# Reordered start of a fused attention and expert kernel: GpSimd's first low half, the maxima of head 1, the gate copy and some routing operations

## Chip, core and metric

One core of a Trainium2 chip runs the whole kernel in one launch. The metric is the device time of one execution in microseconds (us); lower is better.

## What is computed

The reference has three stages: attention with a hashed mask, a mixture of 8 experts with one expert per token and a capacity, and a dense layer with a gated activation.

```python
B, H, S, D = 2, 8, 768, 64
mask = q_bucket[:, :, :, None] == k_bucket[:, :, None, :]   # 6 sign bits of q @ proj, k @ proj
scores = where(mask, q @ k.T / sqrt(D), -1e9)
attn = softmax(scores)
x = (attn @ v)                                              # 1536 tokens x 512
expert = argmax(x @ w_gate); gate = softmax(x @ w_gate)[expert]
y = gate * (relu(x @ w1[expert]) @ w2[expert])              # 512 -> 1024 -> 512, first `cap` tokens
h = y @ w_in                                                # 512 -> 2048
out = (h * clip(h + 3, 0, 6) / 6) @ w_out                   # 2048 -> 512
```

## The kernel before

The order of the work on every engine is written out by hand: instructions stand in each engine's queue in the order in which the program issues them, and each waits for its own operands. Factors are split into a high and a low part (fp16 or a rounded fp32), so a product is a sum of two or three matmuls.

**Attention.** There are 16 heads, each with 6 blocks of 128 keys, so 96 steps `k`. `mx(n)` (L448 to L461) takes two matmuls into one of three PSUM buffers `psm`, each followed on VectorE by a maximum (L457) over 384 keys; after the sixth block of a head, L460 reduces to `top`, and SyncE sends it by DMA into row 76 of `X` (L461), where the scores of that head read it. `scores(k)` (L463) takes four matmuls (L471, L472) into two buffers `pst` and two exponentials on ScalarE (L473) into `pf`. `high(k)` rounds `pf` to fp16 `phi` on ScalarE or VectorE; `low(k)` (L487) subtracts it from `pf` on GpSimd or VectorE to give `plo`. `pv` (L502 to L504) multiplies by the values, 18 matmuls for a block, two blocks in every odd step. A head's maxima run ahead of its scores by some steps: `Q["ac"]` gives how many are issued in each of the first steps (through `AHEAD`).

**The start (ramp).** Before the main loop stand head 0's maxima, the first two score blocks and `vscale(0)` (L601 to L643), a chain of small VectorE operations with two tiny TensorE products in it, which finds the power-of-two scales of the values and of the gate weights. Its last operation writes `isw` (L643). `vsplit(h)` (L715) splits the values of a head: ScalarE L721 and L723, then GpSimd L727 for heads 0 and 1 and VectorE L729 for later ones. `vgate(r)` (L557) brings the products of two heads' values with the gate weights: matmuls into `psg` (L565), a copy to `gv` (L571), two transposes (L575), and four small VectorE operations (L583, L584). `low_half` (L372) is VectorE's low part of a head's queries and keys. `heat` (L335) issues 512-column matmuls whose result nobody reads; `Q["hn"]` tells how many in each of the first steps. `stages(gen, ks)` runs the successive parts of a piece of work at the given times: a part with time `t` is issued by `due`, which is called with `k - 0.5` at the start of step `k` and with `k` at its end.

**The end of attention.** The last maxima are issued in step 87. `route(0)` (L208) and `weigh(0)` (L277), the routing of the first batch's tokens, are spread in 22 and 7 parts among the steps from 66 on: `pos` (L248), `ge` (L251), a count and `jo` (L253, L254), `pl` and `jt` (L257, L259), `rh` (L204), then the one-hot blocks `ohr` (L273).

**Behind attention.** The routing of the second batch, 8 experts (L1099, L1126) and the dense layer (L1348, L1375) follow; nothing of them is changed.

Of the kernel before, what the change touches and what calls it, by code (L numbers as in the profile page):

```python
# [23 lines left out]
NC = S // P  # L24
# [39 lines left out]
def moe_attention_kernel(ctx, tc, qk, v, vt, pj, wg, w1, w2, win, wout, out, cap):  # L64
    nc = tc.nc
    pe, act, dve, pool, sp = nc.tensor, nc.scalar, nc.vector, nc.gpsimd, nc.sync
# [3 lines left out]
    def opened(stack, name, bufs, side="left", **kw):  # L70
        return stack.enter_context(tc.tile_pool(name=name, bufs=bufs, side=side, reuse_waits="tile", **kw))
# [4 lines left out]
    def run(gen):  # L76
        for _ in gen:
            pass
# [4 lines left out]
    def persist(shape, dt, name):  # L83
        return const.tile(shape, dt, tag=name, name=name)
# [14 lines left out]
    isw = persist([P, 1], F32, "isw")  # L99
# [208 lines left out]
                )  # L308


    Q = {'tk': (84, 86), 'v': (-3.25, -4.75, -1.75, -2.25), 'vg': (-6.5, -6.75), 'vgd': 1, 'pr': (-13.0, -12.75, -12.0, -12.5), 'prd': 0.6, 'b0': 7.75, 'b': 1.75, 'bd': 0.5, 'vm0': (9.5, 10.5, 11.5, 12.5), 'vm': (-0.5, 4.75, 7.0, 12.25), 'vs': 13.25, 'pa': 1.5, 'ev': 0.5, 'lvt': -5.0, 'v4': (2.0, 4.25, 10.0, 16.25), 'vg0': (1.85, -4.4, 9.0), 'p2': 3.5, 'lr': (0.25, 1.25, 2.25), 'lv': 4.0, 'vsd': 0.75, 'ac': (1, 1, 3, 5, 6, 7, 8, 10), 'hd': (3, 5, 17), 'hn': (0, 0, 3, 2, 2, 1, 0, 0), 'ap': (0,), 'h0': (7,), 'hl': (6,), 'l0': (), 'll': (1, 3), 'ht': (6, 3, 7, 6, 3, 2)}


    HT = Q["ht"]

    with ExitStack() as actx:
        pa = opened(actx, "pa", 1)
        pr = opened(actx, "pr", 6)
# [4 lines left out]
        ps_v = opened(actx, "ps_v", 2, space=PSUM)  # L323
# [6 lines left out]
        def heat(pool_, tag, n, cols=512):  # L330

            if pool_ not in heat_t:
                heat_t[pool_] = pool_.tile([P, 512], F32, tag=tag, name=f"heat{tag}")
            for _ in range(n):
                pe.matmul(heat_t[pool_][:, :cols], idle_sb[:, 0:P], idle_sb[:, :cols], start=True, stop=True)  # L335
# [19 lines left out]
        def misc(name):  # L355
            return ps_x.tile([P, 512], F32, tag="x", name=name)
# [121 lines left out]
        def high(k, eng):  # L478
            phi_t[k] = pt.tile([P, S], F16, tag="phi", name=f"phi{k}", bufs=6)
            if eng is act:  # L480
                act.activation(phi_t[k], pf_t[k], AF.Copy)  # L481
            else:
                eng.tensor_copy(phi_t[k], pf_t[k])

        def low(k, eng):
            plo_t[k] = pt.tile([P, S], F16, tag="plo", name=f"plo{k}", bufs=5)
            eng.tensor_tensor(out=plo_t[k], in0=pf_t.pop(k), in1=phi_t[k], op=ALU.subtract)  # L487
            if k in Q["tk"]:
                c = plo_t[k][:, 0:1]
# [111 lines left out]
        def vscale(g, fresh=misc):  # L601

            am = am_t.pop(g)
            n = 1 + (g == 0)
            am1 = ph.tile([P, n], F32, tag="am1", name=f"am1{g}")
            dve.tensor_reduce(out=am1[:, 0:1], in_=am, axis=AX.X, op=ALU.max)
            if n > 1:
                dve.tensor_reduce(
                    out=am1[:, 1:2], in_=wg_sb.rearrange("p k h e -> p (k h e)"), axis=AX.X, op=ALU.max,
                    apply_absolute_value=True,  # L610
                )
            yield
            ps = misc(f"psn{g}")
            pe.transpose(ps[0:n, 0:P], am1, ident)
            yield
            am2 = ph.tile([n, 1], F32, tag=f"am2{n}", name=f"am2{g}")
            dve.tensor_reduce(out=am2, in_=ps[0:n, 0:P], axis=AX.X, op=ALU.max)
            if n > 1:
                a, am2 = am2, ph.tile([n, n], F32, tag="dg", name="dg")
                dve.tensor_tensor(out=am2, in0=a.to_broadcast([n, n]), in1=ident[0:n, 0:n], op=ALU.mult)  # L620
            yield
            ps = misc(f"pso{g}")
            pe.matmul(ps[:, 0:n], ones[0:n, :], am2, start=True, stop=True)
            yield

            a = ph.tile([P, n], F32, tag=f"am3{n}", name=f"am3{g}")
            dve.tensor_copy(a, ps[:, 0:n])
            a = a.bitcast(I32)
            x = ph.tile([P, 2 * n - 1], I32, tag=f"ex{n}", name=f"ex{g}")
            sc = sc_t[g] = ph.tile([P, 2 * n - 1], F32, tag=f"sc{n}", name=f"sc{g}", bufs=1 + (n == 1))  # L630
            dve.tensor_scalar(out=a, in0=a, scalar1=23, scalar2=None, op0=ALU.logical_shift_right)
            dve.tensor_scalar(out=a, in0=a, scalar1=15, scalar2=None, op0=ALU.max)
            for i, (j, k, c) in enumerate(((0, -1, 268), (1, -1, 268), (1, 1, 7))[: 2 * n - 1]):
                dve.tensor_scalar(
                    out=x[:, i : i + 1], in0=a[:, j : j + 1], scalar1=k, scalar2=c, op0=ALU.mult, op1=ALU.add
                )
            dve.tensor_scalar(out=sc.bitcast(I32), in0=x, scalar1=23, scalar2=None, op0=ALU.logical_shift_left)
            dve.tensor_copy(vsc[:, g : g + 1], sc[:, 0:1])
            sw_t[g] = ph.tile([P, 1], F32, tag="sw", name=f"sw{g}", bufs=2)
            dve.tensor_scalar(out=sw_t[g], in0=sc[:, 0:1], scalar1=SW, scalar2=None, op0=ALU.mult)  # L640
            if n > 1:
                dve.tensor_scalar(out=wg_sb, in0=wg_sb, scalar1=sc[:, 1:2], scalar2=None, op0=ALU.mult)
                dve.tensor_copy(isw, sc[:, 2:3])  # L643
# [131 lines left out]
        b0 = bits(0, [ps_v.tile([P, 512], F32, tag="v", name=f"psb0{n}") for n in range(2)])  # L775
# [9 lines left out]
        vs = vscale(0)  # L785
# [7 lines left out]
        next(vs)  # L793
        next(vs)
        run(vs)
        heat(ps_v, "v", 2)
        mx(NC)
        run(pre[1])
# [2 lines left out]
        first = vsplit(0), vgate(0)  # L801
# [4 lines left out]
        STEPS = NC * NH  # L806
        AC = (1,) + Q["ac"]
        AHEAD = [range(NC + AC[i], NC + AC[i + 1]) for i in range(8)]
        END = 2 * NC

        def on_dve(k):
            if k < END:
                return k in Q["h0"]
            return k - STEPS + END in Q["hl"] if k >= STEPS - END else k % 24 in Q["hd"]

        def on_pool(k):
            if k < END:
                return k not in Q["l0"]
            return k < STEPS - END or k - STEPS + END in Q["ll"]
# [4 lines left out]
        def at(k, f, *args):  # L824
            later.setdefault(k, []).append((f, args))

        def spread(k, gen, d=1):


            def part(k):  # L830
                if next(gen, gen) is not gen:
                    n = k + (d if k < STEPS - NC * 2 else min(d, 1) * 0.75)
                    at(n, part, n)

            at(k, part, k)

        def stages(gen, ks):
            for k in ks:
                at(k, next, gen, None)

        stages(first[0], (2, 2))
        stages(first[1], (2, 3, 3.5, 4, 4.5))
        at(5.0, run, pre[2])
        for i in range(3):
            at(Q["lr"][i], load_r, 5 + i)
        for g in range(1, G):
            b = 4 * NC * (g - 1)
            spread(b + Q["b"] + (g == 2) if g > 1 else Q["b0"], bits(g), Q["bd"])
            at(b - 6 if g > 1 else Q["lv"], load_v, g)
            for i in range(4):  # L850
                at(b + (Q["vm"] if g > 1 else Q["vm0"])[i], vmax, g, i)
            if g == 1:
                stages(vscale(g), (13, 14.5, 15.25, 16.75, 17.5))
            else:
                spread(b + Q["vs"], vscale(g))
        for h in range(8, NH):
# [8 lines left out]
        for h in range(NH):  # L865
            k = NC * h + NC - 1 + LAG
# [5 lines left out]
            elif h < NH - 1:  # L872
                at(k + Q["pa"], pair, h // 2)
                at(NC * h + (Q["lvt"] if h > 1 else -3.5), load_vt, h // 2 + 1)
        stages(route(0, lambda: misc("psr0")), [66 + 1.5 * i for i in range(8)] + [84.5 + 0.75 * i for i in range(14)])
        stages(weigh(0), (84, 86, 87.25, 88.5, 90.5, 91.5, 92.5))
        stages(any_unmatched(), (88.5, 91, 93.5))
        for i in range(4):
# [10 lines left out]
        for k in range(STEPS + LAG + 2):  # L889
            due(k - 0.5)  # L890
            if 1 < k <= STEPS and not on_dve(k - 1):
                high(k - 1, act)
            if 1 < k < STEPS:
                scores(k)
            if k < 8 and Q["hn"][k]:
                heat(ps_v, "v", Q["hn"][k])
            u = k - 2
            if 0 <= u < STEPS:
                if u not in phi_t:
                    high(u, dve)  # L900
                low(u, pool if on_pool(u) else dve)
            for n in AHEAD[k] if k < len(AHEAD) else (k + LEAD,):
                if n < STEPS:
                    mx(n)
            for u in (k - LAG - 1, k - LAG) if k % 2 else ():
                if 0 <= u < STEPS:
                    pv(u)
            due(k)
# [664 lines left out]
```

## Time and profile before

| what | value |
|---|---|
| runs of the kernel before | 659.13, 660.0, 663.14 us (median 660.0) |
| the profiled execution, its own time | 659.11 us |
| span of the profile | 657.4 us |
| mean granted TensorE clock in the span | 0.987 of full |
| attention steps in the span | from about 15 to 223 us |

The span is counted from the profile's first instruction; all times below are us from there. PE is TensorE, PEld its weight loads, DVE VectorE, ACT ScalarE, POOL GpSimd, SP the queue of SyncE. A row of the timeline gives start, duration, engine, line, operation, output and inputs, the number of instructions merged into the row, and in brackets the idle time of the engine before it with what ended it. The duration of merged rows covers all of them.

### The profile page before, as it was taken

What the parts mean: (1) busy time and instruction counts of PE and PEld (TensorE: products, weight loads), DVE (VectorE), ACT (ScalarE), POOL (GpSimd) and SP (SyncE); (2) the same over time, 40 slices, a digit from 0 to 9 for tenths busy, and PEclk for the clock granted to TensorE, in tenths of its full rate; (3) what the DMA queues carried; (4) which work ended last, traced back from release to release, by engine and by line L of the source; (5) the groups of instructions that cost most, each with busy time, mean ns of one, the idle gap of its engine ahead of it and who ended that gap; (6) DMA issues with size and microseconds to landing.
All of it is one profiled execution on the core that took longest, in us unless ns stands there. A gap on an engine that the chain in (4) does not pass through costs nothing.

```text
span 657.4 us, 14405 instructions
## 1 busy us (share of the span) xinstructions
PE 628.8 (96%) x5512; PEld 469.8 (71%) x5512; DVE 473.0 (72%) x1040; ACT 435.9 (66%) x882; POOL 237.1 (36%) x221
## 2 busy tenths in 40 slices
PE   8899999999999789999999999999999999999892
PEld 3588889889897569999999995555555555555441
DVE  6789888888899888888888887888887332222310
ACT  8768879879877746776777745555545585555820
POOL 6566978888896053120666200000000030000011
PEclk9999999999999999999999999999999999999997
DMA  6556856855465168777677543444441020000011
GB/s 195 154 154 163 243 143 155 249 147 145 114 169 194 28 223 296 248 248 232 213 248 252 193 158 100 143 145 129 137 149 36 1 80 17 1 0 1 1 49 53
DMA packets 37844, 92.19 MB, mean 140 GB/s; under 512 B 8986, under 2 KB 14362, under 8 KB 37762
## 3 DMA queue, kind: packets, MB, share of 16 engines
q1 hardware_dynamic: 34674, 83.75, 42.4%
q0 software_dynamic: 2400, 7.36, 3.3%
q8 instruction: 46, 0.75, 0.5%
q14 instruction: 36, 0.29, 0.1%
q10 hardware_dynamic: 688, 0.03, 0.1%
HBM read 67.14 MB, written 6.29 MB: 112 GB/s over the span
## 4 chain that ended last, share of the span: by engine, by line
PE 56%; ACT 3%; DMA 3%; DVE 1%; issue 1%; POOL 0%; POOLq 0%
PE psg L1348 17%; PE pso L1375 15%; PE psy L1126 11%; PE psh L1099 11%; DMA out_dram<-os,inv 3%; ACT junk L1302 2%; PE psa L1076 1%; ACT gh L1358 1%; DVE rl L1351 1%; PE heat L1178 0%; ACT rl L1350 0%; DVE wl L164 0%; PE heatt L335 0%; POOL out_dram L1390 0%; DVE os L1382 0%
## 5 line engine op out<-in xcount | busy, mean ns | idle before, releaser
L487 POOL TENSOR_TENSOR plo<-pf,phi 128x768 f16<-128x768 f32 x86 | 145.6, 1715 | 23.8 <-ACT phi L481 6.8
L1390 POOL DMA_INDIRECT out_dram<-os,inv x12 | 12.2, 1014 | 272.3 <-DVE os L1382 244.3
L457 DVE TENSOR_REDUCE mx<-psm 128x1 f32<-128x384 f32 x192 | 96.7, 549 | 17.2 <-PE psm L454 16.6
L473 ACT ACTIVATE pf<-pst 128x384 f32<-128x384 f32 x192 | 83.2, 486 | 35.8 <-PE pst L472 32.9
L164 DVE SCALAR_TENSOR_TENSOR wl<-raw,wh 128x1024 f16<-128x1024 f32 (+1 forms) x68 | 82.5, 1216 | 5.6 <-ACT wh L158 5.2
L1348 PE MATMUL psg<-yTh,ch 128*128 128x512 f16 (+1 forms) x256 | 83.4, 326 | 3.2 <-DVE rl L1351 3.2
L1348 PE MATMUL psg<-yTl,ch 128*128 128x512 f16 (+1 forms) x256 | 83.4, 326 | 0.0
L1348 PE MATMUL psg<-yTh,cl 128*128 128x512 f16 (+1 forms) x256 | 83.4, 326 | 0.0
L1351 DVE SCALAR_TENSOR_TENSOR rl<-rl,psg 128x512 f32<-128x512 f32 x64 | 35.0, 551 | 64.4 <-ACT rl L1350 64.0
L471 PE MATMUL pst<-Y,K 128*128 128x384 f32 x192 | 75.0, 391 | 2.6 <-ACT pf L473 2.6
L1348 PEld LDWEIGHTS <-ch 128*128 128x128 f16 x512 | 50.1, 98 | 35.9
L481 ACT ACTIVATE phi<-pf 128x768 f16<-128x768 f32 x85 | 71.7, 844 | 1.9
L1375 PE MATMUL pso<-ch,gh 128*128 128x512 f16 x192 | 72.8, 379 | 0.0
L1375 PE MATMUL pso<-ch,gl 128*128 128x512 f16 x192 | 72.8, 379 | 0.0
L1375 PE MATMUL pso<-cl,gh 128*128 128x512 f16 x192 | 72.8, 379 | 0.0
L1375 PEld LDWEIGHTS <-gh 128*128 128x128 f16 x384 | 37.6, 98 | 42.3
L158 ACT ACTIVATE wh<-raw 128x1024 f16<-128x1024 f32 (+1 forms) x68 | 67.4, 998 | 0.5 <-issue 0.5
L1126 PE MATMUL psy<-hh,wl 128*128 128x224 f16 x256 | 66.3, 259 | 0.0
L1126 PE MATMUL psy<-hh,wh 128*128 128x224 f16 x256 | 66.3, 259 | 0.0
L1126 PE MATMUL psy<-hl,wh 128*128 128x224 f16 x256 | 66.3, 259 | 0.0
L472 PE MATMUL pst<-X,K 77*128 77x384 f32 x192 | 65.9, 343 | 0.3 <-DMA X<-top 0.3
L454 PE MATMUL psm<-K,X 76*128 76x384 f32 x192 | 64.1, 414 | 2.1 <-DVE mx L457 1.5
(247 smaller groups left out, 1495.4 us busy)
## 6 DMA issues: line engine op xcount, KB each, us to landing
raw<-in_w_dram SPq DMA_DIRECT2D x64, 512.0 KB
rc<-in_win_dram SPq DMA_DIRECT2D x16, 512.0 KB
rc<-in_wout_dram SPq DMA_DIRECT2D x16, 512.0 KB
r<-in_qk_dram SPq DMA_DIRECT2D x16, 384.0 KB
K<-hi SPq DMA_DIRECT2D x26, 192.0 KB
vr<-in_v_dram SPq DMA_DIRECT2D x4, 768.0 KB
vt<-in_vt_dram SPq DMA_DIRECT2D x8, 384.0 KB
K<-lo SPq DMA_DIRECT2D x16, 192.0 KB
```

Of the source, the lines that this page charges most:

```text
L158: act.activation(wh[e, i][:, c : c + n], r, AF.Copy, scale=(S1, S2)[i // 2])
L164: dve.scalar_tensor_tensor(out=wl[e, i][:, c : c + n], in0=r, scalar=(S1, S2)[i // 2], in1=wh[e, i][:, c : c + n], op0=ALU.mult, op1=ALU.s ...
L457: dve.tensor_reduce(out=mm[:, c, n : n + 1], in_=ps[:, :HS], axis=AX.X, op=ALU.max)
L471: pe.matmul(ps[:, :HS], st["K1"][:, kc], st["Y"][:, qc], start=True, stop=False)
L472: pe.matmul(ps[:, :HS], st["K2"][0:77, kc], st["X"][0:77, qc], start=False, stop=True)
L473: act.activation(pf.rearrange("k (c n p) -> k c n p", c=NC, n=2)[:, :, n], ps[:, :HS].rearrange("k (p c) -> k c p", c=NC), AF.Exp, scale=0 ...
L481: act.activation(phi_t[k], pf_t[k], AF.Copy)
L487: eng.tensor_tensor(out=plo_t[k], in0=pf_t.pop(k), in1=phi_t[k], op=ALU.subtract)
L1099: pe.matmul(ps, l[:, c], r[:, k], start=n == 0, stop=n == 3 * KD - 1)
L1126: pe.matmul(ps, l, r, start=n == 0, stop=n == 3 * KF - 1)
L1348: pe.matmul(ps, l, x, start=n == 0, stop=n == 3 * KD - 1)
L1375: pe.matmul(po[blk][s], l, r, start=first and n == 0, stop=last and n == 2)
```

## The change

GpSimd gets a copy of `isw` onto itself, issued behind `vscale(0)` and so ahead of `low(0)` in GpSimd's queue. Blocks 7 to 11 of the maxima (the rest of head 1) are issued as one in step 2, two in step 3 and two in step 4, where it was two, two and one. The parts of `vgate(0)` move half a step forward: the copy `gv` from the end of step 3 to its start, the transposes from the start of step 4 to the end of step 3, the first two small operations from the end to the start of step 4. Steps 3 and 4 have one heat matmul where they had two; step 6 gets three, ahead of its scores. `vscale(1)`, `jo` and what follows of `route(0)` are given later times.

```diff
-Q: 'ac': (1, 1, 3, 5, 6, 7, 8, 10), 'hn': (0, 0, 3, 2, 2, 1, 0, 0)
+Q: 'ac': (1, 1, 2, 4, 6, 7, 8, 10), 'hn': (0, 0, 3, 1, 1, 1, 0, 0)
...
         run(vs)
+        pool.tensor_copy(isw, isw)
         heat(ps_v, "v", 2)
...
         stages(first[0], (2, 2))
-        stages(first[1], (2, 3, 3.5, 4, 4.5))
+        stages(first[1], (2, 2.5, 3, 3.5, 4.5))
...
             if g == 1:
-                stages(vscale(g), (13, 14.5, 15.25, 16.75, 17.5))
+                stages(vscale(g), (13, 15, 15.75, 17, 17.75))
...
-        stages(route(0, lambda: misc("psr0")), [66 + 1.5 * i for i in range(8)] + [84.5 + 0.75 * i for i in range(14)])
+        stages(route(0, lambda: misc("psr0")), [66 + 1.5 * i for i in range(8)] + [84.5, 85.25, 87.25, 87.75] + [88.25 + 0.67 * i for i in range(10)])
...
             due(k - 0.5)
             if 1 < k <= STEPS and not on_dve(k - 1):
                 high(k - 1, act)
+            if k == NC:
+                heat(ps_v, "v", 3)
             if 1 < k < STEPS:
                 scores(k)
```

## Rows read from the trace of the kernel before

**Rows 1.** Windows: stretch, length, busy PE, PEld, DVE, ACT, POOL, granted clock, DMA share, GB/s

```profile
45.00:60.00 15.00, 14.55 (x177) 13.16 (x176) 14.05 (x38) 13.40 (x25) 12.48 (x9) 1.00 0.47 120
...
150.00:200.00 50.00, 49.45 (x610) 44.88 (x610) 44.07 (x108) 42.88 (x81) 44.98 (x38) 1.00 0.62 160
...
29.90:33.30 3.40, 3.40 (x23) 2.70 (x23) 3.01 (x9) 3.33 (x7) 2.15 (x2) 0.50 0.17 23
```

**Rows 2.** Timeline of VectorE, 19 to 35 us

```profile
19.35 1.14 DVE L631 TENSOR_SCALAR am<-am 128x2 int32<-128x2 int32 x1
20.53 0.17 DVE L632 TENSOR_SCALAR am<-am 128x2 int32<-128x2 int32 x1
...
21.63 2.87 DVE L457 TENSOR_REDUCE mx<-psm 128x1 f32<-128x384 f32 x6
...
25.85 1.95 DVE L457 TENSOR_REDUCE mx<-psm 128x1 f32<-128x384 f32 x4 [1.32 <-PE psm L454]
27.72 0.41 DVE L571 COPY gv<-psg 96x256 f32<-96x256 f32 x1
...
31.03 0.17 DVE L460 TENSOR_REDUCE top<-mx 128x6 fp32r<-128x18 f32 x1
31.12 0.26 DVE L583 TENSOR_SCALAR vh<-psg,sw 128x48 f16<-128x48 f32 x1
...
33.31 1.16 DVE L372 SCALAR_TENSOR_TENSOR lo<-r,hi 128x768 fp32r<-128x768 f32 x1
```

**Rows 3.** Timeline of GpSimd, 18 to 34 us

```profile
18.81 1.66 POOL L487 TENSOR_TENSOR plo<-pf,phi 128x768 f16<-128x768 f32 x1 [3.50 <-ACT phi L481]
22.59 0.89 POOL L727 TENSOR_TENSOR vh<-vr,vh 128x384 f16<-128x384 f32 x1 [2.12 <-ACT vr L723]
23.44 4.89 POOL L487 TENSOR_TENSOR plo<-pf,phi 128x768 f16<-128x768 f32 x3
...
32.01 1.65 POOL L487 TENSOR_TENSOR plo<-pf,phi 128x768 f16<-128x768 f32 x1
```

**Rows 4.** Timeline of TensorE, 22 to 39 us

```profile
22.23 1.48 PE L454 MATMUL psm<-K,X 76*128 76x384 f32 x3 [0.62 <-DVE mx L457]
23.64 0.63 PE L565 MATMUL psg<-vt,wg_sb 128*32 128x256 f32 x6
24.20 0.44 PE L471 MATMUL pst<-Y,K 128*128 128x384 f32 x1
...
25.03 0.61 PE L335 MATMUL heatv<-idle_sb 128*128 128x512 f16 x2
...
28.19 0.38 PE L575 MATMUL psg<-ident,gv 96*128 96x96 f32 x2 [1.17 <-DVE gv L571]
...
30.08 0.52 PE L471 MATMUL pst<-Y,K 128*128 128x384 f32 x1
...
34.07 0.42 PE L471 MATMUL pst<-Y,K 128*128 128x384 f32 x1
...
37.59 0.21 PE L502 MATMUL psv<-vh,phi 128*128 128x73 f16 x1
...
38.82 0.42 PE L471 MATMUL pst<-Y,K 128*128 128x384 f32 x1
```

**Rows 5.** Timeline, head 0's `top` sent by SyncE and first read

```profile
14.03 0.52 SPq L461 DMA_DIRECT2D X<-top  x1
16.11 0.41 PE L472 MATMUL pst<-X,K 77*128 77x384 f32 x1 [0.31 <-DMA X<-top]
```

**Rows 6.** Timeline of TensorE, `vscale(1)`'s transpose

```profile
54.47 0.27 PE L614 MATMUL psn<-ident,am 128*1 128x128 f32 x1 [0.45 <-DVE vh L584]
```

**Rows 7.** Timeline of VectorE and GpSimd, 203 to 213 us

```profile
204.41 1.03 DVE L254 TENSOR_TENSOR jo<-ge 128x24 f32<-128x24 f32 x1
...
203.74 1.65 POOL L487 TENSOR_TENSOR plo<-pf,phi 128x768 f16<-128x768 f32 x1
209.19 0.19 POOL L490 COPY plo<-plo 128x1 f16<-128x1 f16 x1 [3.79 <-DVE plo L487]
```

More of the change, by code (lines that the diff above doesn't have):

```diff
@@ L308, in windows @@
                 )
-    Q = {'tk': (84, 86), 'v': (-3.25, -4.75, -1.75, -2.25), 'vg': (-6.5, -6.75), 'vgd': 1, 'pr': (-13.0, -12.75, -12.0, -12.5), 'prd': 0.6, 'b0': 7.75, 'b': 1.75, 'bd': 0.5, 'vm0': (9.5, 10.5, 11.5, 12.5), 'vm': (-0.5, 4.75, 7.0, 12.25), 'vs': 13.25, 'pa': 1.5, 'ev': 0.5, 'lvt': -5.0, 'v4': (2.0, 4.25, 10.0, 16.25), 'vg0': (1.85, -4.4, 9.0), 'p2': 3.5, 'lr': (0.25, 1.25, 2.25), 'lv': 4.0, 'vsd': 0.75, 'ac': (1, 1, 3, 5, 6, 7, 8, 10), 'hd': (3, 5, 17), 'hn': (0, 0, 3, 2, 2, 1, 0, 0), 'ap': (0,), 'h0': (7,), 'hl': (6,), 'l0': (), 'll': (1, 3), 'ht': (6, 3, 7, 6, 3, 2)}
+    Q = {'tk': (84, 86), 'v': (-3.25, -4.75, -1.75, -2.25), 'vg': (-6.5, -6.75), 'vgd': 1, 'pr': (-13.0, -12.75, -12.0, -12.5), 'prd': 0.6, 'b0': 7.75, 'b': 1.75, 'bd': 0.5, 'vm0': (9.5, 10.5, 11.5, 12.5), 'vm': (-0.5, 4.75, 7.0, 12.25), 'vs': 13.25, 'pa': 1.5, 'ev': 0.5, 'lvt': -5.0, 'v4': (2.0, 4.25, 10.0, 16.25), 'vg0': (1.85, -4.4, 9.0), 'p2': 3.5, 'lr': (0.25, 1.25, 2.25), 'lv': 4.0, 'vsd': 0.75, 'ac': (1, 1, 2, 4, 6, 7, 8, 10), 'hd': (3, 5, 17), 'hn': (0, 0, 3, 1, 1, 1, 0, 0), 'ap': (0,), 'h0': (7,), 'hl': (6,), 'l0': (), 'll': (1, 3), 'ht': (6, 3, 7, 6, 3, 2)}
     HT = Q["ht"]
```

## The prediction

> **What bounds the kernel now.** I read the windows first. From 45 us to the end of attention TensorE is busy 97 to 99% of the time at full clock, with VectorE second at 94% early on [rows 1]. So work taken off another engine is worth nothing there, but time won before 45 us moves everything behind it, since the order of the work stays the same. What counts is therefore when step 6's scores start, the first matmul of head 1's scores: 34.07 us now [rows 4]. I then read the timelines of VectorE, GpSimd and TensorE side by side from 18 to 35 us, and VectorE's again at the end of attention. Four losses can be seen in them.
>
> First, L631, a shift of 128x2 integers, takes 1.14 us where its neighbour L632 takes 0.17 [rows 2]. It began at 19.35 while GpSimd's `low(0)` ran from 18.81 to 20.47 [rows 3] and ended as that ended. The six maxima of head 1 that are queued behind the chain start only at 21.63 [rows 2]. Second, the matmuls of the gate products stand behind four maxima matmuls in TensorE's queue; these wait for PSUM buffers, so the gate products start at 23.64 and step 3's scores at 24.20 [rows 4]. VectorE then has nothing to do for 1.32 us before the next maxima at 25.85 [rows 2]. Third, the copy `gv` waits behind those four maxima until 27.72 [rows 2], TensorE's transposes wait 1.17 us for it, and step 4's scores stand behind the transposes [rows 4]. Fourth, TensorE's granted clock is 0.50, the lower level of 1.2 GHz, from 29.90 to 33.30 [rows 1], right after that idle stretch; a score matmul takes 0.52 us there [rows 4].
>
> **The ramp, step by step.** I follow the path anew with the same durations.
>
> *The scale's chain.* With GpSimd's copy in front of `low(0)`, L631 should take 0.17: 1.14 - 0.17 = 0.97 us sooner, and the first maximum starts at 21.63 - 0.97 = 20.66. A maximum takes 2.87 / 6 = 0.48 [rows 2].
>
> *What waits behind the copy.* The copy waits for L643, which would end at about 20.7. Behind it in GpSimd's queue stand `low(0)`, then the low half of head 0's values (L727), then the next lows. `low(0)` would run from about 20.9 to 22.6. L727 started at 22.59, after 2.12 us of idleness, because ScalarE's input came only then [rows 3]; this idleness is the cover and is just used up. The copy has no row of its own; the nearest is a GpSimd copy of 128x1 at 0.19 us [rows 7]. On the path it costs between 0 (the cover holds) and 0.2; I take 0. If the cover were gone, the three lows at 23.44 [rows 3] would move, and the first values' products with them.
>
> *Fewer maxima in step 2.* Block 7's second matmul needs the buffer of block 6's first maximum: 20.66 + 0.48 + about 0.1 (22.11 to 22.23 in rows 2 and 4) = 21.25. With only block 7 in this step, the gate products follow at about 21.6 rather than 23.64, and step 3's scores at 21.6 + 0.6 = 22.2 rather than 24.20.
>
> *Gate copy.* Block 7's maxima end at 20.66 + 4 x 0.48 = 22.6. Scores of one step take 24.20 to 25.03 = 0.83 and a heat matmul 0.61 / 2, less overlap about 0.22 [rows 4], so block 8's first maximum can start at 22.2 + 0.83 + 0.22 + 0.39 = 23.6, where 0.39 is 25.85 less the end of the two heat matmuls (25.03 + 2 x 0.215 = 25.46). `gv` with its 0.41 [rows 2] fits into VectorE's gap between 22.6 and 23.6. Its cost is nothing while that gap is there; else 0.41. The transposes then find it done, and the wait of 1.17 goes.
>
> *What is late next.* VectorE: blocks 8 and 9 from 23.6 (4 x 0.48 = 1.9), the first two small gate operations (0.26 each [rows 2], 0.5), blocks 10 and 11 (1.9), then `top` (0.17 [rows 2]): 23.6 + 4.5 = 28.1, against 31.20 now. SyncE's transfer of `top` was issued at 14.03 and read at 16.11 [rows 5], 2.1 us, so head 1's row is there at 30.2. TensorE: the last matmul of block 11 waits for block 10's first maximum, until 26.6; step 5's scores 26.8 to 27.6, one heat matmul 0.2, block 12 0.45, the 36 products with the values 37.59 to 38.82 = 1.23 [rows 4], the three new heat matmuls 0.65: step 6's scores start at 30.2. The new heat stands just where the row of `top` would be waited for. It costs between 0 and 0.65, and I take 0.2, the part that the landing would not have covered. The gain at step 6 is 34.07 - 30.2 = 3.9 us. It contains 0.97 of the chain, about 1 of the gate products, 1.2 of the transposes' wait and some 1.6 of the slow clock, less what VectorE's row of maxima then sets; with the clock at its upper level, 3.4 us at half speed shrink to 1.7.
>
> *Port.* `low_half` of head 2 (L372) took 1.16 us at 33.31, where GpSimd's low of 32.01 + 1.65 ended at 33.66 [rows 2, 3]: it waited 0.35. It now comes at about 29.5, when GpSimd has just begun `low(4)` at 29.3, so it may wait until 31.0, 1.5 us on VectorE. The next maxima matmuls have three buffers to run ahead in, and block 14's second one would be some 0.2 us late. Bounds 0 and 1.5; I take 0.2, as only the buffer that runs out reaches TensorE. Ramp: 3.7 us.
> The Trainium skill, SBUF — State Buffer, "Who interferes with whom", says that a VectorE instruction with two SBUF inputs contends with a GpSimd instruction that reads SBUF, and that the later one "fully blocks". By that, the sum has the 1.5 us on VectorE as above; without it, 0. The two waits above (L631's and L372's) agree with it.
>
> **The other edits.** `vscale(1)`: TensorE waits 0.45 us at 54.47 before its transpose [rows 6]; a half step later VectorE's input is done. Bounds 0 and 0.45, I take 0.4. Its last operations come a quarter step later, far ahead of head 4's values, which cost nothing. End of attention: VectorE runs there without a gap. `jo` took 1.03 us at 204.41 [rows 7] beside GpSimd's low (203.74 to 205.39); L632's 0.17 [rows 2] is the nearest small operation without such a neighbour. Behind the last maxima it would start at about 204.4 + 2 x 0.48 + 0.3 for `top` and the count = 205.7, when that low is over: 0.86 gained. On the other hand `pl`, `jt` and `rh` now stand behind `low(86)`, between it and the operations that GpSimd's copies wait for; three small operations of 0.1 to 0.17 take some 0.3 back, an estimate. Bounds 0 and 1.1 (the chain of VectorE, ScalarE and GpSimd moving as a whole); if `jo` met a GpSimd instruction again, nothing would be won. I take 0.6.
>
> **Sum.** 3.7 + 0.4 + 0.6 = 4.7 us. The profiled execution took 659.1 us (span 657.4 and 1.7 around it), so 654.4. The median of the runs shown is 660.0, 0.9 above it; I carry that over: 655.3 us, 0.7% less.
>
> **Rivals.**
>
> *The clock still falls.* Steps 3 and 4 lose a heat matmul each, and TensorE still waits some 0.4 us around 24 and 0.6 around 26. Against it: the waits that preceded the fall were 1.17 and longer in all, and TensorE's queue is denser by the same work in less time. If one slow stretch stays, 1.7 us go: 657.0. Chance 0.13.
> The Trainium skill, TensorE: Matmul & The Clock Gate, "What's actually happening", says that "the default state is throttled, and activity releases the throttle". By that, taking heat away is a risk where waits remain, and the sum would lose the 1.7 us.
>
> *Given back later.* VectorE is busy 14.05 of 15 us between 45 and 60, and GpSimd 44.98 of 50 between 150 and 200 [rows 1]; with the waits gone, GpSimd's lows meet VectorE's two-input operations at other places. For it speaks L372 above; against it, that the same order moves as a whole. Were half of the ramp lost so, 1.9 us: 657.2. Chance 0.14.
>
> *The chain stays long.* If L631's 1.14 us were not GpSimd's doing, 0.97 us would be missing and GpSimd would start at 21.8, L727 1 us late: 656.3. Against it, the ends of the two agree. Chance 0.05.
>
> *Slower.* Place: TensorE between 23 and 33 us. If the clock were low in three stretches like the one of rows 1 rather than none, each would cost 1.7 us, 5.1 in all; with 4.7 of gain the time would be 660.4. It decides from the third stretch on, and half of the time of steps 3 to 8 would have to run at 1.2 GHz. Nothing in the timeline makes the queue that thin. Chance 0.03.
>
> *More than forecast.* The mean granted clock of 0.987 in the table of times is lower than one stretch of rows 1 makes it, so there are other slow stretches, and moving all work by 4 us and more can move it out of one: 1.7 us less by the price above, 653.6; with the tail's bound at its good end, 653.1. Chance 0.07.
>
> **How the numbers follow.** Forecast 0.58, and the rivals 0.13, 0.14, 0.05, 0.03, 0.07 in their order. The range of 8 in 10 has to reach to the two likely rivals and their spread, up to 658.6, and down to 652.8: heat, port and tail at their good ends give 0.2 + 0.2 + 0.5 = 0.9, and most of the last rival's 1.7 on top. A measurement of this kernel tells about 1% from no change, 6.6 us. Faster than 653.4 takes the last rival or the good end of the forecast: 0.12. Slower by 1% would need more than the slower rival: 0.02. The rest, 0.86, is within 1%.
>
> **What would show it.** Right: L631 takes 0.17 us; step 6's scores start near 30.2; the granted clock stays full between 20 and 45; `gv` runs before block 8's maxima; L614 doesn't wait; `jo` takes about 0.2. The forecast is wrong if the first matmul of step 6 is early by 3 to 4 us but the last products with the values are not; if the clock shows 0.50 between 22 and 34; or if the three lows of GpSimd at 23.44 start later than 24.

## The result and the profile after

| | before | changed |
|---|---|---|
| median of the runs | 660.04 us | 653.86 us |
| lowest to highest | 657.58 to 663.14 | 651.75 to 654.53 |
| ratio, 95% interval | | 0.9902 [0.9874, 0.9931] |
| profiled execution, its time / span | 659.11 / 657.4 us | 653.03 / 651.3 us |
| mean granted clock in the span | 0.987 | 0.993 |

The forecast was 655.3 us with a range of 652.8 to 658.6. The measured 653.86 us lies in the range, 6.2 us below the median of before, where 4.7 were forecast. In the changed kernel the lines up to L795 have the numbers of before; those behind are shifted by one to three.

VectorE's timeline in the changed kernel, beside [rows 2]:

```profile
19.20 0.17 DVE L631 TENSOR_SCALAR am<-am 128x2 int32<-128x2 int32 x1
...
20.50 2.03 DVE L457 TENSOR_REDUCE mx<-psm 128x1 f32<-128x384 f32 x4
22.46 0.41 DVE L571 COPY gv<-psg 96x256 f32<-96x256 f32 x1
...
23.62 1.95 DVE L457 TENSOR_REDUCE mx<-psm 128x1 f32<-128x384 f32 x4 [0.74 <-PE psm L454]
25.48 0.26 DVE L583 TENSOR_SCALAR vh<-psg,sw 128x48 f16<-128x48 f32 x1
...
26.13 1.95 DVE L457 TENSOR_REDUCE mx<-psm 128x1 f32<-128x384 f32 x4
28.11 0.17 DVE L460 TENSOR_REDUCE top<-mx 128x6 fp32r<-128x18 f32 x1
...
29.62 1.86 DVE L372 SCALAR_TENSOR_TENSOR lo<-r,hi 128x768 fp32r<-128x768 f32 x1
```

L631 is down from 1.14 to 0.17 us. The gate copy `gv` sits in the gap between two groups of maxima, and `top` ends at 28.3 where it ended at 31.2. GpSimd's timeline, beside [rows 3]:

```profile
20.65 0.19 POOL L796 COPY isw<-isw 128x1 f32<-128x1 f32 x1 [5.23 <-DVE isw L643]
20.80 1.64 POOL L487 TENSOR_TENSOR plo<-pf,phi 128x768 f16<-128x768 f32 x1
22.48 0.89 POOL L727 TENSOR_TENSOR vh<-vr,vh 128x384 f16<-128x384 f32 x1
23.33 4.88 POOL L487 TENSOR_TENSOR plo<-pf,phi 128x768 f16<-128x768 f32 x3
...
29.02 3.98 POOL L487 TENSOR_TENSOR plo<-pf,phi 128x768 f16<-128x768 f32 x2
```

`low(0)` comes 2 us later, and what stands behind it no later than before (22.48 and 23.33; 22.59 and 23.44 before). The cover was just used up. TensorE's timeline, beside [rows 4]:

```profile
21.64 0.63 PE L565 MATMUL psg<-vt,wg_sb 128*32 128x256 f32 x6
22.20 0.44 PE L471 MATMUL pst<-Y,K 128*128 128x384 f32 x1
...
24.62 0.33 PE L575 MATMUL psg<-ident,gv 96*128 96x96 f32 x2
...
27.14 0.34 PE L471 MATMUL pst<-Y,K 128*128 128x384 f32 x1
...
29.71 0.81 PE L335 MATMUL heatv<-idle_sb 128*128 128x512 f16 x3
30.17 0.52 PE L471 MATMUL pst<-Y,K 128*128 128x384 f32 x1
...
35.02 0.42 PE L471 MATMUL pst<-Y,K 128*128 128x384 f32 x1
```

The transposes (L575) no longer wait, and step 6's scores start at 30.17 where they started at 34.07. The windows of the changed kernel, columns as in [rows 1], show the clock at its upper level throughout the ramp and no idleness of TensorE behind it:

```profile
20.00:25.00 5.00, 4.80 (x28) 3.39 (x27) 4.22 (x14) 4.71 (x9) 4.30 (x5) 1.00 0.84 296
25.00:30.00 5.00, 4.81 (x54) 4.03 (x54) 4.81 (x14) 4.32 (x8) 5.00 (x4) 1.00 0.28 102
30.00:35.00 5.00, 4.80 (x53) 4.13 (x52) 4.45 (x8) 3.09 (x6) 4.57 (x3) 1.00 0.84 247
...
45.00:60.00 15.00, 15.00 (x178) 13.92 (x176) 14.18 (x38) 13.08 (x25) 10.77 (x8) 1.00 0.60 155
```

`vscale(1)`'s transpose L614, which waited 0.45 us [rows 6], has no wait left. At the end of attention `jo` starts behind the last maxima and takes 0.18 us where it took 1.03 [rows 7]:

```profile
201.12 0.18 DVE L254 TENSOR_TENSOR jo<-ge 128x24 f32<-128x24 f32 x1
```

**Where the time went.** The start of each step's scores (first L471 of the step, as in [rows 4]) can be read in every profile. Counted from step 2's scores of the same execution and set against the same count in the kernel before, the changed kernel gains, in us:

| step | 4 | 6 | 8 | 14 | 15 | 16 | 20 | 50 | 91 | 92 | 95 |
|---|---|---|---|---|---|---|---|---|---|---|---|
| changed | -3.47 | -3.75 | -3.65 | -3.64 | -4.27 | -4.03 | -4.79 | -4.73 | -4.37 | -5.10 | -5.10 |

So 3.65 us come from the ramp, 0.4 at steps 15 and 16 and 0.75 at step 20 (the second scale), 0.73 at step 92 (the routing), and 0.4 are lost little by little between steps 20 and 91. Another 0.15 were gained ahead of step 2, whose scores start at 19.76 instead of 19.91, so step 95 stands 5.25 us sooner in the span. Behind attention 0.78 of this go: the dense layer's first matmul stands at 387.69 against 392.16, 4.5 us sooner, and so does the last result on VectorE (637.35 against 641.82). Of the 0.78, 0.27 go ahead of the first expert, 0.42 in it and 0.10 later. They are not shown to be the change's: from step 95 to the dense layer the profile of before has 174.03 us and that of after 174.82, and over all fourteen profiles shown here (two of the changed kernel) the stretch lies between 173.8 and 175.3; the four variants of the kernel before have 174.6 to 175.3. The other 1.6 us of the profiles' difference of 6.1 lie behind the last result: from there to the end of the span the profile of before has 15.57 us, that of after 13.96. The runs below come back to this.

### The profile page after: what moved, and what is told of

It is laid out like the page before. It is cut to its first block, busy times and chain, and to the rows that moved or that the text cites. A ratio compares the mean times of both kernels' runs of the same rounds, so it can differ in the third digit from the quotient of the medians.

```text
span 651.3 us, 14410 instructions
## 1 busy us (share of the span) xinstructions
PE 627.0 (96%) x5513; PEld 468.8 (72%) x5513; DVE 472.9 (73%) x1040; ACT 435.4 (67%) x882; POOL 235.6 (36%) x222
## 4 chain that ended last, share of the span: by engine, by line
PE 56%; ACT 3%; DMA 2%; DVE 2%; issue 1%; POOL 0%; POOLq 0%; ACTq 0%
PE psg L1351 17%; PE pso L1378 16%; PE psy L1129 11%; PE psh L1102 11%; DMA out_dram<-os,inv 2%; ACT junk L1305 2%; PE psa L1079 1%; ACT gh L1361 1%; DVE rl L1354 1%; DVE wl L164 1%; ACT rl L1353 0%; ACT wh L158 0%; PE heat L1181 0%; DVE sum L974 0%; DVE hl L1106 0%
## 5 line engine op out<-in xcount | busy, mean ns | idle before, releaser
L471 PE MATMUL pst<-Y,K 128*128 128x384 f32 x192 | 75.0, 391 | 2.2 <-ACT pf L473 2.2
L472 PE MATMUL pst<-X,K 77*128 77x384 f32 x192 | 65.6, 342 | 0.3 <-DMA X<-top 0.3
```

Source lines behind the costliest of these rows:

```text
L471: pe.matmul(ps[:, :HS], st["K1"][:, kc], st["Y"][:, qc], start=True, stop=False)
L472: pe.matmul(ps[:, :HS], st["K2"][0:77, kc], st["X"][0:77, qc], start=False, stop=True)
```

## The experiments

All were made from the kernel before or the changed one, and gains by step use the count above. All but the two that are said to be timed are one execution each, so they are judged by steps inside the profile; the whole time of one execution shows little, since six executions of the changed kernel already lie between 651.75 and 654.53.

**GpSimd's copy alone** (kernel before).

```diff
         run(vs)
+        pool.tensor_copy(isw, isw)
```

> The kernel before with GpSimd's copy alone. Theory (the port): L631 takes 0.17 us, head 1's maxima start 1.0 us sooner, and all that follows moves with them: step 6's scores at 33.1 and step 8's at 37.8, against 34.07 and 38.82 before; the clock still falls, as nothing else of the queue has changed. Rival (the chain is hidden): L631 is short, but the wait for the gate copy takes the microsecond back, and step 6 starts at 34.0 as before. Second rival (L631 is long for a reason of its own): it stays at 1.14 us.

Measured: 0.88 us gained at step 3 and still 0.88 at step 19; 657.84 us. L631 is short, nothing takes the gain back, and the other losses stay. TensorE's timeline of this kernel still has the wait for the gate copy and a slow matmul after it:

```profile
26.99 0.39 PE L575 MATMUL psg<-ident,gv 96*128 96x96 f32 x2 [1.17 <-DVE gv L571]
...
29.40 0.52 PE L471 MATMUL pst<-Y,K 128*128 128x384 f32 x1
```

**The changed kernel without the copy.**

```diff
-        pool.tensor_copy(isw, isw)
```

> The changed kernel without GpSimd's copy. Theory: L631 is back at about 1.1 us, maxima start at 21.5, and step 6's scores at 31.1 where the changed kernel has 30.17, so the copy is worth 0.9 us also beside the other edits. Rival: the other edits leave enough slack behind the chain, and step 6 stays within 0.3 of 30.17.

Measured: step 8 gains 2.49 instead of 3.65, so the copy is worth 1.16 beside the other edits; 657.79 us. On VectorE's timeline of this kernel L631 is long again:

```profile
19.19 1.33 DVE L631 TENSOR_SCALAR am<-am 128x2 int32<-128x2 int32 x1
```

GpSimd's `low(0)` ran there from 18.84 to 20.50, and L631 ended as it ended. With the run before, this shows from both sides that GpSimd's low half holds up the scale's chain. Later this execution lost 1.1 us each at steps 51 and 84, where nothing was edited; the last section comes back to that.

**Two, two and one maxima blocks** (changed kernel).

```diff
-'ac': (1, 1, 2, 4, 6, 7, 8, 10)
+'ac': (1, 1, 3, 5, 6, 7, 8, 10)
```

> The changed kernel with two, two and one maxima blocks in steps 2 to 4. Theory of the prediction: fewer maxima ahead of the gate products are worth most of a microsecond, so the gate products start at 22.5 where the changed kernel has 21.64, and step 6's scores near 31. Rival: VectorE's maxima and head 1's row set step 6, and they end at 28.1 to 28.3 in either order: step 6 stays within 0.3 of 30.17.

Measured: step 3 gains 0.89 instead of 1.85, step 4 2.51 instead of 3.47, but step 6 gains 3.75 and step 8 3.65, both as in the changed kernel; 654.25 us. The rival holds. VectorE's timeline of this kernel: `top` ends at 28.55, 0.27 later than in the changed kernel, in an execution whose step 2 started 0.23 later.

```profile
20.74 2.95 DVE L457 TENSOR_REDUCE mx<-psm 128x1 f32<-128x384 f32 x6
23.61 0.41 DVE L571 COPY gv<-psg 96x256 f32<-96x256 f32 x1
24.81 1.95 DVE L457 TENSOR_REDUCE mx<-psm 128x1 f32<-128x384 f32 x4 [0.79 <-PE psm L454]
27.32 1.02 DVE L457 TENSOR_REDUCE mx<-psm 128x1 f32<-128x384 f32 x2
28.38 0.17 DVE L460 TENSOR_REDUCE top<-mx 128x6 fp32r<-128x18 f32 x1
```

**The gate copy where it was** (changed kernel), without and with heat in the wait that this makes (the last line of the diff stands in the second kernel only).

```diff
-        stages(first[1], (2, 2.5, 3, 3.5, 4.5))
+        stages(first[1], (2, 3, 3.5, 4, 4.5))
+        at(3.45, heat, ps_v, "v", 6)
```

> The changed kernel with the gate copy and its transposes where they were. Theory: the copy waits behind block 9's maxima until 25.5, the transposes until 26, step 4's scores start at 26.1 where the changed kernel has 24.73, and step 6's at 31.5 if the clock stays up, near 33 if the longer wait pulls it to 0.50 as in the kernel before. Rival: VectorE's maxima go ahead as before and step 6 is late by less than 0.5.

> The changed kernel with the gate copy and the transposes where they were and six heat matmuls in the stretch in which TensorE then waits for the copy. Theory: with the clock held, what is left of the loss is the order alone, 1.4 us: counted from step 2, step 8's scores are 1.4 us later than in the changed kernel, where they were 4.4 later with the clock at 0.50. Rival: the clock falls in spite of the heat, or the order alone costs 3 us and more.

Measured: without heat step 8 gains nothing and loses 0.78, so it is 4.43 us later than in the changed kernel; 661.24 us, of which 2.25 were lost ahead of step 2, with the clock at 0.50 from 10.1 to 17.0, before the edit acts. With heat step 8 gains 1.74, 1.91 less than in the changed kernel, where 1.4 were expected; 655.72 us. At steps 4 and 6 the loss is 1.37 and 1.70; the last 0.2 come with L372, which took 2.38 us here and 1.86 in the changed kernel. So the place of the copy is worth 1.7 us by order at step 6 and 1.9 at step 8, and the slow clock that follows its wait another 2.5. The windows of the kernel without heat:

```profile
27.00:30.40 3.40, 2.17 (x11) 1.57 (x10) 1.77 (x5) 1.29 (x4) 3.40 (x3) 1.00 0.63 230
30.40:34.00 3.60, 3.45 (x18) 2.75 (x19) 3.22 (x11) 3.37 (x6) 2.65 (x3) 0.53 0.07 8
34.00:37.30 3.30, 3.30 (x36) 2.65 (x34) 1.25 (x3) 0.00 (x0) 1.80 (x1) 0.50 0.92 286
```

TensorE stood still for a third of 27.0 to 30.4, and then ran at 1.2 GHz (0.50) until 37.5, twice as long as in the kernel before. In the kernel with heat the clock is 1.00 in all windows from 20 to 45 us.

**Heat in the wait of the kernel before**, its order kept.

```diff
+        at(3.45, heat, ps_v, "v", 6)
```

> The kernel before with six heat matmuls put into the stretch in which TensorE waits for the gate copy. The order of all other work stays. Theory: the wait makes the clock fall, and the slow stretch alone costs 1.6 us; with the heat the clock stays full and step 6's scores start at 32.4 where they started at 34.07. Rival: the clock's fall is hidden behind VectorE's maxima and the row of head 1, and step 6 stays within 0.4 of 34.07 at full clock. Second rival: the clock falls all the same.

Measured: the clock stays full, as the windows of this kernel show; step 6 gains 1.05, step 8 0.85, half of what was expected.

```profile
26.00:30.00 4.00, 3.81 (x19) 2.36 (x19) 2.27 (x5) 1.55 (x4) 2.47 (x2) 1.00 0.26 99
30.00:33.40 3.40, 3.28 (x46) 2.70 (x45) 3.16 (x10) 3.34 (x7) 2.09 (x2) 1.00 0.15 17
```

What was left on the path can be read on VectorE and TensorE of this kernel:

```profile
31.19 0.17 DVE L460 TENSOR_REDUCE top<-mx 128x6 fp32r<-128x18 f32 x1
...
31.57 0.27 DVE L584 SCALAR_TENSOR_TENSOR vh<-psg,sw,vh 128x48 f16<-128x48 f32 x1
```

```profile
31.59 0.19 PE L502 MATMUL psv<-vh,phi 128*128 128x73 f16 x1
31.90 0.21 PE L503 MATMUL psv<-vh,phi 128*128 128x72 f16 x1
...
33.48 0.42 PE L472 MATMUL pst<-X,K 77*128 77x384 f32 x1
```

`top` comes no sooner than in the kernel before (31.03 [rows 2]). The products with the values (L503) wait for L584, which stands behind it on VectorE, and the first matmul of step 6 that reads `top`'s row (L472) starts 2.1 us behind `top`'s end, as long as that transfer took for head 0 [rows 5]. So with the clock held, VectorE's row of maxima and `top` are on the path. The run's 659.97 us show nothing of the gain: 1.5 us were lost again between steps 51 and 86 (below).

**No heat ahead of step 6, and none in steps 2 to 6** (changed kernel; the last two lines of the diff stand in the second only).

```diff
-            if k == NC:
-                heat(ps_v, "v", 3)
-'hn': (0, 0, 3, 1, 1, 1, 0, 0)
+'hn': (0, 0, 0, 0, 0, 0, 0, 0)
```

> The changed kernel without the three heat matmuls ahead of step 6's scores. Theory: they stand where the row of head 1's maxima is waited for, so the first matmul of step 6 starts 0.6 us sooner, the one that reads the row where it did, and step 7's scores start at 31.5 as in the changed kernel; the clock stays full. Rival: they cost 0.6 us, and step 7 starts at 30.9. Second rival: they hold the clock, and without them it falls to 0.50 between 30 and 37.

> The changed kernel without any heat matmul in steps 2 to 6. Theory: TensorE's queue is dense enough in the changed order, the clock stays full from 20 to 45 us, and step 8's scores start within 0.5 us of 35.02. Rival: the heat holds the clock; without it there is a stretch at 0.50 between 22 and 34, and step 8's scores start 1.5 us or more later.

Measured: without the three, step 6 starts 0.48 sooner (4.23 against 3.75), waits 0.28 us for the row of `top`, and step 8 gains 3.72, as the changed kernel within 0.07; 652.31 us. They cost 0.07 at most and, in this execution, held nothing. Without any heat the clock was 1.00 from 20 to 45 us, step 8 gained 4.10 and step 95 5.35 (5.10 changed); 651.87 us. So the heat of steps 2 to 5 cost some 0.4 at step 8. Both theories that call the heat idle hold so far.

**The same without heat, and the changed kernel, timed in five rounds each.**

> The changed kernel without heat matmuls in steps 2 to 6, timed. Theory: the clock stays full in most executions and the time is 0 to 0.5 us less than the changed kernel's, so 653.4 to 653.9 where that takes 653.9. Rival: in some executions the clock falls, and the median is 1 us or more above the changed kernel's.

> The changed kernel once more, for the comparison with the one without heat and for the time behind attention. Both theories expect a ratio near 0.990 and steps as in its first profile, within 0.3 us; if the 1.6 us between the last result and the end of the span belong to the change, they come again, if they are the output transfers' own scatter, the stretch is anywhere between 13.9 and 15.6 us.

Measured: without heat 653.87 us, ratio 0.9895 [0.9867, 0.9923]; changed 654.68 us, ratio 0.9913 [0.9886, 0.9941]. The intervals overlap, so neither is shown to be better. The changed kernel's second profile repeats its steps within 0.2 us to step 92 (step 8 3.64, step 95 5.29). The one without heat, the same program as in the run above, gained only 0.25 at step 14, because of this on VectorE:

```profile
29.35 3.81 DVE L372 SCALAR_TENSOR_TENSOR lo<-r,hi 128x768 fp32r<-128x768 f32 x1
```

beside this on GpSimd:

```profile
29.07 3.28 POOL L487 TENSOR_TENSOR plo<-pf,phi 128x768 f16<-128x768 f32 x2
```

and, in consequence, this on TensorE and in the windows (the clock stays at 0.50 until 40.2):

```profile
33.70 1.63 PE L454 MATMUL psm<-K,X 76*128 76x384 f32 x3 [1.27 <-DVE mx L457]
```

```profile
33.40:36.00 2.60, 2.30 (x17) 1.76 (x18) 2.57 (x6) 2.13 (x4) 1.09 (x1) 0.50 0.60 156
36.00:38.00 2.00, 2.00 (x28) 2.00 (x26) 0.96 (x1) 0.00 (x0) 0.56 (x1) 0.50 0.51 111
```

Head 2's low half waited for two lows of GpSimd in a row where it waits for one in the changed kernel's profile (29.62 to 31.48). Whether heat would have held the clock through the 1.27 us that follow was not tried.

The stretch from the last result to the end was 15.29 us in the changed kernel's second profile against 13.96 in its first, so the same program has both. Over the fourteen profiles it lies between 13.92 and 15.65, in the kernel of before and its four variants between 15.0 and 15.6. The output's transfers are issued by GpSimd, each behind the landing of the one before; the last two of these waits were 2.89 and 4.58 us in the profile of before, 2.52 and 3.71 in that of after. The 1.6 us are thus within what these transfers vary from execution to execution. The four stretches near 14.0 are all of the changed kernel or its variants without some heat; whether the change makes short ones likelier stays open.

**The second scale's chain alone** (kernel before).

```diff
-                stages(vscale(g), (13, 14.5, 15.25, 16.75, 17.5))
+                stages(vscale(g), (13, 15, 15.75, 17, 17.75))
```

> The kernel before with the later times of the second scale's chain alone. Theory of the prediction: 0.45 us of TensorE's wait at step 15 goes and nothing else, so steps 15 to 95 are 0.4 us sooner. Rival, from the profile of the changed kernel: the chain's last operations no longer stand ahead of the maxima in step 20, so another 0.7 us goes there, 1.1 in all from step 20 on.

Measured: from step 14 to step 16 the run gains 0.40 us, and from step 19 to step 20 another 0.77, so the rival holds. The whole run, 663.88 us, tells nothing of it: this execution had slow stretches of the clock ahead of step 2 and again in the ramp. VectorE's timeline of this kernel:

```profile
64.82 2.05 DVE L729 SCALAR_TENSOR_TENSOR vh<-vr,sc,vh 128x384 f16<-128x384 f32 x1
...
66.81 0.56 DVE L457 TENSOR_REDUCE mx<-psm 128x1 f32<-128x384 f32 x1
67.28 0.55 DVE L457 TENSOR_REDUCE mx<-psm 128x1 f32<-128x384 f32 x1
67.75 0.15 DVE L627 COPY am<-pso 128x1 f32<-128x1 f32 x1
```

In the kernel before the chain's small operations stood between L729 and the next maxima:

```profile
60.44 2.08 DVE L729 SCALAR_TENSOR_TENSOR vh<-vr,sc,vh 128x384 f16<-128x384 f32 x1
62.45 0.14 DVE L627 COPY am<-pso 128x1 f32<-128x1 f32 x1
...
63.51 1.01 DVE L457 TENSOR_REDUCE mx<-psm 128x1 f32<-128x384 f32 x2
```

L729 still takes 2 us beside GpSimd's low halves, but the next maxima now go ahead of the chain's seven small operations.

**The routing operations alone** (kernel before).

```diff
-[84.5 + 0.75 * i for i in range(14)]
+[84.5, 85.25, 87.25, 87.75] + [88.25 + 0.67 * i for i in range(10)]
```

> The kernel before with the later times of the routing operations alone. Theory: jo no longer meets GpSimd's low, takes about 0.2 us where it took 1.03, and steps 92 to 95 are 0.7 us sooner than steps 80 to 86 are, as in the changed kernel. Rival: the gain in the changed kernel comes from where the earlier edits had moved the two engines' instructions against each other; alone it gives less than 0.3.

Measured: from step 91 to step 92 the run gains 0.72 us, as the changed kernel (0.73). But in this execution 1.6 us had been lost by step 86, and its 659.9 us are those of the kernel before. VectorE's timeline of this kernel, the loss and the gain:

```profile
194.37 1.98 DVE L729 SCALAR_TENSOR_TENSOR vh<-vr,sc,vh 128x384 f16<-128x384 f32 x1
...
207.01 0.17 DVE L254 TENSOR_TENSOR jo<-ge 128x24 f32<-128x24 f32 x1
```

## Why the prediction was right

*The ramp* was forecast at 3.7 us and gave 3.65; step 6's scores were forecast at 30.2 and start at 30.17, the gate products at 21.6 and start at 21.64, `top`'s end at 28.1 and comes at 28.28. The method, one path rebuilt with the durations of before, held. The prices that the prediction put on its parts did not all hold:

- *The scale's chain*, 0.97: shown by both runs on the copy, 0.88 alone and 1.16 beside the rest. The rival "the chain stays long" falls. The prediction took L631's wait as agreeing with what it cites on instructions with two inputs; L631 has one, so that it waits for GpSimd rests on the two runs.
- *What waits behind the copy*, nothing: right, with L727 at 22.48.
- *Fewer maxima in step 2*: the step as put, that the gate products come sooner, is right, but what it is worth, "about 1 of the gate products", is not. Taken back alone it costs 0.00 at step 8, since VectorE's row of maxima and `top` set step 6 in either order. The prediction had named that row as what is late next, and did not ask whether this edit moves it.
- *Gate copy*: right in direction, undersized. Its order is worth 1.7 us at step 6 and 1.9 at step 8, where the wait of 1.17 was counted.
- *Clock*: the price of "some 1.6" failed. Holding the clock in the kernel before gains 0.85 at step 8, half of it: TensorE's matmuls were not alone on the path in the slow stretch, since `top` and what waits for it come no sooner. With the old gate copy in the changed kernel the clock is worth 2.5, so a part's price depends on the order that it is taken out of. The mis-sized terms did no harm, because the forecast was not their sum but their joint end, step 6, worked out on the path.
- *The new heat*, 0.2: it costs 0.07 at step 8.
- *Port*, 0.2 of bounds 0 and 1.5: L372 took 1.86 us at 29.62, and step 8 is 0.1 us less early than step 6. By the Trainium skill, SBUF — State Buffer, "Who interferes with whom", the later instruction "fully blocks"; this trace agrees, with GpSimd's low from 29.02. But the bound of one low was too small: in the second run without heat L372 took 3.81.

*The second scale*, 0.4, gave 0.4 where it was looked for and 0.75 at step 20, which failed: the prediction said that the later last operations cost nothing, and did not ask whether they free anything. The row that would have told was VectorE's around 60 us, where the chain stood between L729 and a pair of maxima.

*The end of attention*, 0.6, gave 0.73, shown by the run on the routing alone.

*Given back later*: 0.4 us between steps 20 and 91 (0.3 in the second profile) and 0.8 behind attention, which the sum did not have. With them the terms are 0.15 + 3.65 + 0.4 + 0.75 + 0.73 - 0.4 - 0.8 = 4.5, the shift of the last result, beside a forecast of 4.7. That the two lie so close is luck in part: 0.75 at step 20 that was not forecast stands against 1.2 lost, and the 0.8 is no more than executions differ by in that stretch. The medians differ by 6.2 us here and by 5.1 in the second timing (659.76 and 654.68); the profiles account for 4.5 of it. The rest is of the size of the output transfers' spread, 1.7 us; how much of it is the change's was not settled.

*The clock still falls* did not happen in the ramp of either profile of the changed kernel. *More than forecast* named 653.6 and the measured 653.86 is near it, but not by its cause: of the other slow stretches of before, that behind attention (227.9 to 231.3) is there in both profiles of the changed kernel (223.0 to 226.4 and 223.4 to 226.8), and that from 647.7 on lies behind TensorE's last matmul, which ends at 645.7.

## What to carry to other kernels

Rebuild the path to the first point behind which the engine that bounds the kernel has no gaps, and read every edit at that point; parts priced one by one along the way count waits that hide one another. A wait of TensorE for another engine can cost TensorE's clock as well as the time of the wait (here 1.9 us by order and 2.5 by the clock), so look first for the copy or transpose that is needed soonest and issued last. Where two engines hold each other up, as GpSimd's low half and VectorE's scale chain do, put the long instruction behind the chain of short ones, and judge an edit of under 1 us by milestones inside the profile, since whole runs of one kernel differ by more (2.8 us here).

## What was not expected of the hardware

With the same order on every engine, times came out differently by a microsecond and more, by whether VectorE's instruction or GpSimd's next low half went first. Near step 83 it was the one that came first. In ten profiles, those of before and after among them, L729 started 1.45 to 1.47 us ahead of step 83's scores, 0.15 ahead of GpSimd's next low, and took 0.61 or 0.62. In the other four (without the copy, heat in the wait of the kernel before, the second scale alone, routing alone) the low started 0.07 to 0.10 ahead of L729, L729 took 1.97 to 2.00, and each of these four lost 1.1 us between steps 83 and 84. GpSimd's three lows at this place, in the kernel before and in that with the routing alone:

```profile
190.76 5.20 POOL L487 TENSOR_TENSOR plo<-pf,phi 128x768 f16<-128x768 f32 x3 [1.46 <-PE pst L472]
```

```profile
191.05 4.88 POOL L487 TENSOR_TENSOR plo<-pf,phi 128x768 f16<-128x768 f32 x3 [1.46 <-DVE phi L483]
```

In the first, the third low took 0.33 longer, as L729 (193.83 to 194.44) went ahead of it; in the second it went through, and L729 (from 194.37) ended behind it, at 196.35. In the run with the routing alone nothing had been edited ahead of this place, so a shift of 0.25 us between the two engines, of whatever cause, is worth 1.1 us here. In the ramp the order of coming did not always decide: L372 of head 2 took 2.19 us in one execution of the kernel without heat and 3.81 in the other, where GpSimd's second low, from 30.68, ran ahead of the VectorE instruction that had been waiting since 29.35; in five other profiles, that first execution among them, a waiting L372 went ahead of that low. Why it did not there stays open. A late load can cost as much: without the copy, TensorE waited 0.3 us for queries and keys at step 51, and 1.1 us were lost there.

The clock fell in different places in executions whose work was alike: ahead of step 2 in two of the fourteen profiles, behind attention in nine, and in the ramp of the kernel without heat once of twice. By the Trainium skill, TensorE: Matmul & The Clock Gate, "What's actually happening", "the default state is throttled, and activity releases the throttle"; these profiles agree that a fall follows a wait (27.0 to 30.4 above). They show besides that the same wait does not bring it each time: behind attention TensorE stood idle for 2.55 to 3.10 us at the same place in all fourteen; after 2.55 us the clock fell in one profile (the old gate copy with heat) and stayed up in two others (without the copy, and the second without heat).
